# One 128-row tile for the last query rows of two heads, in an attention and mixer kernel

## The chip, the cores and the metric

The kernel runs on one core of one Trainium2 chip. The metric is the device time of one execution in microseconds (us); the median of the runs is what is compared.

## The reference

Causal attention with a forget-gate bias, then two mixers on its output. B = 4 batches, H = 8 heads, S = 576 positions, D = 64.

```python
cum  = np.cumsum(np.maximum(s, 0.0), axis=-1)
bias = -(cum[:, :, :, None] - cum[:, :, None, :])
scores = np.where(causal, -1e9, q @ k.T / np.sqrt(D) + np.minimum(bias, 0.0))
attn = np.exp(scores - scores.max(-1)); attn /= attn.sum(-1) + 1e-9
x = attn @ v                                  # [B, S, 512]
xk, xr = mu * x + (1 - mu) * x_prev           # one mu each
y = sigmoid(xr @ w_r) * (np.maximum(xk @ w_k, 0) ** 2 @ w_v)
u = y + (np.maximum(y.T @ w_tok1, 0) @ w_tok2).T
out = u + np.maximum(u @ w_ch1, 0) @ w_ch2
```

All data are float32.

## The kernel before

Products are made in the fp32r format of TensorE: a number is split into a high part (fp32r) and a low part, and two or three matmuls stand for one.

**Attention.** The 576 query rows of a head are five tiles: four of 128 rows (j = 0 to 3) and a last one of 64 (j = 4, `TAIL` = 64). Batch 0 goes through other functions (`early`, `late`) that the change leaves alone, but for one view. Batches 1 to 3 are 24 "visits" of one head each, and a pair (visit i, i + 1, i even) shares its loads. An "item" (i, j) is one query tile: `scores` (L286) makes two matmuls for each part of the row (L296 and L297; for j = 4 the 576 keys are two parts of 288), DVE masks them and takes the row maximum while it copies them to SBUF (L271), ACT makes the exponential (L281), POOL and DVE the reciprocal of the sum (L282, L283), and POOL scales the row (L284). `transposes` (L411) turns P in blocks of 128 keys (L421), ACT writes the high part of the result (L449 into `PT`), DVE the low part (L450). `values` (L452) multiplies with the split V in two passes: c = 0 for query rows 0 to 255 after j = 1, and c = 1 for rows 256 to 575 (`CM` = 320 columns) after j = 4; its matmuls are on L473. ACT and DVE then write the result into `xt` (L479, L480).

**Buffers.** Three PSUM tiles for scores (`ps_s`), two for transposes (`ps_t`), one for values (`ps_v`). `PT` has one buffer for the high and one for the low part, `X1`, `X2` (operands of the scores) one for even and one for odd visits. q and k of a pair come raw in four pieces (`load`, L228), are split into `HL` by ACT (L75) and POOL (L235) in `split`, and go from there by DMA to the operands of a visit in `place` (L261 to L264). `HL` has one buffer. V of a pair comes raw into `VS` in three DMAs (`load_v`, L240 and L242) after the tail of the even visit, and is split by DVE (L77) and POOL (L253) in `split_v` in the odd visit. These DMAs, and the stores of the mixer (L539), are all issued by SP, one after the other.

**Order.** Every piece of work has a place on a line of priorities, `at(N0 + n + ...)`, with n the number of the item; scores at n, transposes at n + 1.5, values at n + 2. The matmuls of the first mixer (`up`, `gate`, `down`; 40 units a batch, L107 through `products`) are dealt out over the items: batch 0's second half over the items of batch 1, batch 1's over those of batch 2, and so on, from the third item of a batch at the earliest. A scheduler takes the pieces by priority when its own timeline says they are ready, and so fixes the order on each engine before the run. After the last item come the mixer of batch 3 and the second mixer, which is TensorE work almost without a break.

Of the kernel before, what the change touches and what calls it, by code (L numbers as in the profile page):

```python
# [8 lines left out]
F32 = mybir.dt.float32  # L9
# [15 lines left out]
def attention_moe_mixer(  # L25
# [29 lines left out]
    QC = 256  # L55
# [71 lines left out]
    VS = v_p.tile([128, NS, 2 * D], F32, name="VS")  # L127
# [3 lines left out]
    FIRST = QC + 128  # L131
    BLK = [CM * k for k in range(NS - 1)] + [CM * (NS - 2) - (128 * (NS - 1) - QC)]
# [6 lines left out]
    def pt_tile(slot, dtype=F32):  # L139
        return pt_p.tile([128, (NS - 1) * CM], dtype, tag=f"PT{slot}", name=f"PT{slot}")  # L140
# [8 lines left out]
    def constants():  # L149
# [4 lines left out]
        make_identity(nc, ident)  # L154

# [47 lines left out]
    items = [(i, j) for i, (g, js, w) in enumerate(visits) for j in js]  # L203
# [33 lines left out]
    def load_v(i):  # L237
        b, h = divmod(visits[i][0], H)
        n = S // 128
        nc.sync.dma_start(out=VS[:, 0:n], in_=v[b, 0:128 * n, h * D:(h + 2) * D].rearrange("(t p) d -> p t d", p=128))  # L240
        for r in (0, TAIL):
            nc.sync.dma_start(out=VS[r:r + TAIL, n], in_=v[b, 128 * n:S, h * D:(h + 2) * D])  # L242

    def split_v(i):
        y = (i // 2) % 2
        if i < 4:
            VV[y] = v_tile(y, F32R)
        for t0, t1 in ((0, NS // 2), (NS // 2, NS)):
            hi = VV[y][:, t0:t1].rearrange("p t (x d) -> p t x d", d=D)[:, :, 0:4:3, :]
            lo = VV[y][:, t0:t1, D:3 * D].rearrange("p t (e d) -> p t e d", d=D)  # L250
            vs = VS[:, t0:t1].rearrange("p t (e d) -> p t e d", d=D)
            copy("D", hi, vs)
            nc.gpsimd.tensor_tensor(out=lo, in0=vs, in1=f32(hi), op=ALU.subtract)  # L253
# [14 lines left out]
    def softmax_max(j, ps, P, mx, x, c0, c1):  # L268
        m = min(128, S - 128 * j)
        q0 = 128 * j  # L270
        nc.vector.tensor_tensor_reduce(  # L271
            out=P[0:m, c0:c1], in0=ps[0:m, 0:c1 - c0], in1=maskc[0:m, 512 - q0 + c0:512 - q0 + c1],
# [4 lines left out]
    def softmax(j, P, mx, x):  # L277
        m = min(128, S - 128 * j)
        w = 128 * j + m
        sm = st_p.tile([128, 2], F32, tag="sum", name="sum")  # L280
# [5 lines left out]
    def scores(i, j):  # L286
        m = min(128, S - 128 * j)
        w = 128 * j + m
        x1, x2 = xs(i)
# [3 lines left out]
        parts = [(0, w)] if w <= 512 else [(0, w // 2), (w // 2, w)]  # L293
# [117 lines left out]
    def transposes(i, j):  # L411
# [23 lines left out]
        for r, k0, k1 in ((128, 0, nf), (TAIL, nf, nk)):  # L435
            if k0 == k1:
                continue
# [571 lines left out]
```

## Time and profile before

| What | us |
|---|---|
| Median of three runs (878.01 to 887.47) | 878.74 |
| The profiled execution | 877.69 |
| Its span, first to last instruction | 875.9 |
| PE busy, DVE, ACT, POOL | 846.1, 498.7, 460.7, 355.1 |
| First and last L296 matmul (scores of batches 1 to 3) | 121.1, 418.7 |

The span is cut by the profile into what each engine does. PE is TensorE's matmuls, PEld its weight loads, DVE the vector engine, ACT the scalar engine, POOL GpSimd, SP the engine that only issues DMAs; "SPq" and "PEq" are an engine's sequencer. A matmul's recorded duration runs from its start to the modelled end of its way through the array, so durations overlap: what a matmul costs in a stream is the step from its start to the next one's start.

### The profile page before, as it was taken

The numbers are of one execution on the slowest core, as the hardware profiler recorded it, in microseconds if no ns is written. First come the engines' busy times: TensorE is split into PE (matmuls) and PEld (weight loads), VectorE is DVE, ScalarE is ACT, GpSimd is POOL, SyncE is SP. The second block draws the span as 40 slices with busy tenths as digits, with TensorE's granted clock in tenths as the row PEclk, the third lists the DMA queues.
The fourth block names the chain that finished last, engine by engine and source line by source line (L and its number), as shares of the span: only waits on it lengthen the run. The fifth ranks groups of instructions, "written<-read, shape, count | busy, mean of one in ns | idle before, by whom it ended". The sixth has DMA issues, their size and how long they took to land.

```text
span 875.9 us, 17584 instructions
## 1 busy us (share of the span) xinstructions
PE 846.1 (97%) x6129; PEld 787.6 (90%) x6129; DVE 498.7 (57%) x1423; ACT 460.7 (53%) x1304; POOL 355.1 (41%) x622
## 2 busy tenths in 40 slices
PE   7999999998899999989999899999999999999998
PEld 5657779996799999989999899899999999999998
DVE  4878866667888657896469766961331222222221
ACT  3989757766877856769376774840310211211210
POOL 3765656755766745756256764730000000000000
PEclk7999999999989999999999999999999999999999
DMA  7953545556654536542234655562022112112100
GB/s 198 260 149 92 148 107 122 117 136 141 139 118 102 106 91 135 118 104 43 66 103 130 213 164 182 189 195 94 12 85 58 41 36 68 43 37 68 42 25 25
DMA packets 74888, 94.19 MB, mean 108 GB/s; under 512 B 10304, under 2 KB 58432, under 8 KB 74800
## 3 DMA queue, kind: packets, MB, share of 16 engines
q1 hardware_dynamic: 68352, 77.40, 34.1%
q0 software_dynamic: 4576, 15.08, 5.5%
q8 instruction: 49, 0.80, 0.4%
q10 hardware_dynamic: 1872, 0.59, 0.3%
q14 instruction: 39, 0.32, 0.1%
HBM read 56.50 MB, written 14.75 MB: 81 GB/s over the span
## 4 chain that ended last, share of the span: by engine, by line
PE 72%; DMA 8%; DVE 6%; issue 6%; ACT 4%; POOL 4%; SPq 1%; POOLq 0%; DVEq 0%; ACTq 0%
PE c L107 33%; PE h L107 8%; PE vd L107 6%; PE r L107 4%; PE t L421 3%; PE pv L473 3%; PE t L107 3%; PE pv L407 2%; PE s L378 2%; DMA X<-HL 2%; PE s L296 2%; PE s L297 2%; DMA raw<-in_moe_w_ch_dram 1%; DVE raw L596 1%; PE idle L162 1%
## 5 line engine op out<-in xcount | busy, mean ns | idle before, releaser
L848 ACT ACTIVATE HID<-c 128x256 fp32r<-128x256 f32 (+1 forms) x96 | 39.3, 410 | 220.6 <-PE c L107 220.5
L284 POOL TENSOR_SCALAR P<-P,sum 64x576 f32<-64x576 f32 (+4 forms) x160 | 102.9, 646 | 43.1 <-DVE sum L283 30.5
L107 PE MATMUL vd<-KK,WV 128*128 128x256 f32 (+1 forms) x768 | 120.1, 300 | 0.0
L107 PE MATMUL h<-XK,WK 128*128 128x320 f32 (+1 forms) x672 | 110.8, 307 | 2.8 <-ACT k L507 2.8
L281 ACT ACTIVATE P<-P,mx 64x576 f32<-64x576 f32 (+4 forms) x160 | 96.2, 603 | 27.8 <-DVE mx L271 24.9
L107 PEld LDWEIGHTS vd<-KK,WV 128*128 128x128 f32 x768 | 106.0, 188 | 3.4 <-issue 0.9
L107 PE MATMUL c<-HID,WV 128*128 128x256 f32 (+1 forms) x768 | 104.8, 291 | 0.0
L107 PE MATMUL c<-U,WK 128*128 128x256 f32 (+1 forms) x768 | 103.2, 292 | 0.6 <-DVE HID L849 0.6
L107 PEld LDWEIGHTS c<-HID,WV 128*128 128x128 f32 x768 | 100.6, 188 | 0.0
L107 PEld LDWEIGHTS h<-XK,WK 128*128 128x128 f32 x672 | 95.6, 192 | 5.5 <-ACT k L507 4.0
L107 PEld LDWEIGHTS c<-U,WK 128*128 128x128 f32 x768 | 98.6, 188 | 0.9 <-DVE HID L849 0.9
L849 DVE SCALAR_TENSOR_TENSOR HID<-c,HID 128x256 fp32r<-128x256 f32 (+1 forms) x96 | 43.8, 456 | 81.1 <-ACT HID L848 81.0
L913 DVE TENSOR_TENSOR ut<-c,ut 128x256 f32<-128x256 f32 (+1 forms) x32 | 14.7, 458 | 119.3 <-PE c L107 104.7
L271 DVE CUSTOM_DVE_ANT_0 P<-s,maskc 64x288 f32<-64x288 f32 (+4 forms) x160 | 74.3, 472 | 13.4 <-PE idle L162 4.4
L510 POOL TENSOR_TENSOR KK<-k,KK 128x256 fp32r<-128x256 f32 (+1 forms) x64 | 56.3, 882 | 12.3 <-ACT k L509 10.7
L107 PE MATMUL r<-XR,WR 128*128 128x320 f32 (+1 forms) x384 | 60.3, 299 | 0.0
L282 POOL TENSOR_SCALAR sum<-sum 128x1 f32<-128x1 f32 (+1 forms) x160 | 35.5, 222 | 60.2 <-ACT P L281 50.0
L421 PE MATMUL t<-ident,P 128*128 128x128 f32 (+1 forms) x360 | 53.4, 263 | 4.3 <-DVE PT L450 2.4
L107 PE MATMUL c<-HID,WR 128*128 128x256 f32 (+1 forms) x384 | 54.8, 291 | 0.0
L107 PEld LDWEIGHTS r<-XR,WR 128*128 128x128 f32 x384 | 52.7, 189 | 0.2
L107 PE MATMUL c<-U,C1A 128*128 128x256 f32 (+1 forms) x384 | 52.8, 296 | 0.0
L235 POOL TENSOR_TENSOR HL<-qkr,HL 128x288 f32<-128x288 f32 x48 | 40.2, 848 | 30.8 <-ACT HL L75 30.4
(122 smaller groups left out, 1685.4 us busy)
## 6 DMA issues: line engine op xcount, KB each, us to landing
X<-HL SPq DMA_DIRECT2D x72, 288.0 KB
raw<-in_moe_w_ch_dram POOLq DMA_DIRECT2D x48, 256.0 KB, 3.5
qkr<-in_qk_dram SPq DMA_DIRECT2D x48, 144.0 KB
yt<-y_d SPq DMA_DIRECT2D x16, 288.0 KB
u_d<-yt SPq DMA_DIRECT2D x16, 288.0 KB
raw<-in_moe_w_k_dram SPq DMA_DIRECT2D x8, 512.0 KB
raw<-in_moe_w_v_dram SPq DMA_DIRECT2D x16, 256.0 KB
ut<-u_d SPq DMA_DIRECT2D x32, 128.0 KB
```

What stands on the lines that cost most here:

```text
L107: nc.tensor.matmul(ps, a, b, start=first and i == 0, stop=last and i == n - 1)
L235: nc.gpsimd.tensor_tensor(out=lo, in0=t, in1=hi, op=ALU.subtract)
L271: nc.vector.tensor_tensor_reduce(out=P[0:m, c0:c1], in0=ps[0:m, 0:c1 - c0], in1=maskc[0:m, 512 - q0 + c0:512 - q0 + c1], scale=-scale, sca ...
L281: nc.scalar.activation(out=P[0:m, 0:w], in_=P[0:m, 0:w], func=AF.Exp, bias=mx[0:m, x:x + 1], scale=-1.0, accum_out=sm[0:m, 0:1])
L282: nc.gpsimd.tensor_scalar(out=sm[0:m, 0:1], in0=sm[0:m, 0:1], scalar1=1e-9, scalar2=1.0, op0=ALU.add, op1=ALU.mult)
L284: nc.gpsimd.tensor_scalar(out=P[0:m, 0:w], in0=P[0:m, 0:w], scalar1=sm[0:m, 1:2], scalar2=1.0, op0=ALU.mult, op1=ALU.mult)
L296: nc.tensor.matmul(ps[0:m, 0:c1 - c0], x1[:, 0, q0:q0 + m], x1[:, 1, c0:c1], start=True, stop=False)
L421: nc.tensor.transpose(ps[0:r, p0 + m * k:p0 + m * k + m], P[0:m, 128 * k:128 * k + r], ident[0:m, 0:m])
L473: nc.tensor.matmul(ps[:, o:n], vv[:, k, :], part, start=(k == 0 and t == 0), stop=(k == nk - 1 and t == len(parts) - 1),)
L510: nc.gpsimd.tensor_tensor(out=kk[:, 1, m, 0:n], in0=t[:, 0:n], in1=f32(kk[:, 0, m, 0:n]), op=ALU.subtract)
L848: nc.scalar.activation(out=hi, in_=ps, func=AF.Relu)
L849: nc.vector.scalar_tensor_tensor(out=lo, in0=ps, scalar=0.0, in1=f32(hi), op0=ALU.max, op1=ALU.subtract)
```

## The change

It touches batches 1 to 3 alone, apart from three small instructions at the start.

- The two 64-row tiles of a pair become one tile of 128 rows, worked at the even visit's j = 4: rows 0 to 63 are the even head's last queries, rows 64 to 127 the odd head's. The odd visit has four items. There are 108 items, and the mixer units are dealt out over them.
- Its scores come in parts of 512 and 64 keys instead of two of 288. For each part the odd head's two matmuls write 128 rows (its last 128 queries), then the even head's two overwrite rows 0 to 63.
- The 64 keys of the second part have a mask of their own, `maskp`, made at the start by a memset and a copy on POOL and a DMA on ACT's queue.
- One transpose of 128 x 128 for each of four key blocks, and one for the last 64 keys, into a PSUM tile of its own.
- A row of `PT` is 384 wide instead of 320 (`PW`): even tail, j = 2, j = 3, odd tail. Each head reads 320 of it. For the even head the block k = 3 comes in two pieces (64 and 128 columns) for each part, so its c = 1 pass has 11 matmuls instead of 9, and the result goes to `xt` in two DVE instructions.
- Raw V comes in two parts, key blocks 0 and 1, then 2 to 4, through a `VS` of three blocks instead of five. Part 0 is loaded at the even visit's j = 2 and split at its j = 4, behind that the load of part 1 is issued, and part 1 is split at the odd visit's j = 2.

```diff
-    VS = v_p.tile([128, NS, 2 * D], F32, name="VS")
+    VS = v_p.tile([128, (NS + 1) // 2, 2 * D], F32, name="VS")
+    maskp = v_p.tile([128, TAIL], BF16, name="maskp")
+    PW = CM + TAIL
-        return pt_p.tile([128, (NS - 1) * CM], dtype, tag=f"PT{slot}", name=f"PT{slot}")
+        return pt_p.tile([128, (NS - 1) * PW], dtype, tag=f"PT{slot}", name=f"PT{slot}")
+        nc.gpsimd.memset(maskp, 0.0)
+        nc.gpsimd.tensor_copy(maskp[0:TAIL], maskc[0:TAIL, 512:512 + TAIL])
+        nc.scalar.dma_start(out=maskp[TAIL:2 * TAIL], in_=maskc[0:TAIL, 512:512 + TAIL])
-    items = [(i, j) for i, (g, js, w) in enumerate(visits) for j in js]
+    items = [(i, j) for i in range(len(visits)) for j in range(NS - i % 2)]
+    PER = len(items) // (B - 1)
-    def load_v(i):
+    def load_v(i, c):
...
-    def split_v(i):
+    def split_v(i, c):
...
     def scores(i, j):
-        parts = [(0, w)] if w <= 512 else [(0, w // 2), (w // 2, w)]
+        parts = [(0, 128 * j), (128 * j, w)] if pair else [(0, w)]
         for x, (c0, c1) in enumerate(parts):
             ps = ps_s.tile([128, 512], F32, tag="s", name="s")
+            for e in (1, 0) if pair else (0,):
+                x1, x2 = xs(i + e)
+                n, a = (TAIL * (1 + e), S - TAIL * (1 + e)) if pair else (128, q0)
+                nc.tensor.matmul(ps[0:n, 0:c1 - c0], x1[:, 0, a:a + n], x1[:, 1, c0:c1], start=True, stop=False)
+                nc.tensor.matmul(ps[0:n, 0:c1 - c0], x2[:, 0, a:a + n], x2[:, 1, c0:c1], start=False, stop=True)
...
     def transposes(i, j):
+        if j == NS - 1:
+            tail = ps_t.tile([128, 512], F32, tag="t", name="t")
+            nc.tensor.transpose(tail[0:TAIL, 0:128], P[:, 128 * j:128 * j + TAIL], ident)
...
     def values(i, c):
+            todo = [(k, t[:, PW * k + f:PW * k + f + CM], 0) for k in range(NS - 2) for t in PT.values()]
+            for t in PT.values():
+                if e:
+                    todo.append((NS - 2, t[:, z + 3 * TAIL:z + PW], 2 * TAIL))
+                else:
+                    todo.append((NS - 2, t[:, z:z + TAIL], 0))
+                    todo.append((NS - 2, t[:, z + 3 * TAIL:z + CM], 3 * TAIL))
+            todo.append((NS - 1, PT[0][:, z + TAIL + f:z + 2 * TAIL + f], (CM - TAIL) * e))
...
+                    if j == 2:
+                        load_v(i + 2, 0)
                     if j == NS - 1:
-                        load_v(i + 2)
+                        split_v(i + 2, 0)
+                        load_v(i + 2, 1)
...
+            if j == 2:
                 with at(N0 + n + 0.3):
-                    split_v(i + 1)
+                    split_v(i + 1, 1)
...
-            if j == NS - 1:
+            if j == NS - 1 - i % 2:
                 values(i, 1)
```

## Rows read from the trace of the kernel before

**Rows 1.** Stretches of 25 us: busy time (count) by engine, clock, DMA share, GB/s.

```profile
200.00:225.00 25.00, 20.92 (x129) 17.60 (x129) 19.63 (x72) 18.03 (x53) 16.12 (x33) 0.93 0.55 128
225.00:250.00 25.00, 22.69 (x154) 20.81 (x154) 19.02 (x67) 20.78 (x64) 19.54 (x36) 0.86 0.68 153
...
350.00:375.00 25.00, 22.00 (x178) 20.68 (x177) 21.77 (x64) 18.67 (x59) 19.07 (x32) 1.00 0.51 117
```

**Rows 2.** A stretch counted for the mixers' matmuls (L107) alone: PE, PEld, clock, DMA.

```profile
210.00:227.00 17.00, 0.51 (x3) 0.36 (x3) 0.90 0.52 121
```

**Rows 3.** PE's waits, 175 to 430 us: total us, times, longest.

```profile
PE s L296 <- DVE mx L271: 3.1, 5, 1.6
PE pv L473 <- DVE xt L480: 2.8, 3, 1.6
PE t L421 <- DVE PT L450: 2.4, 2, 2.1
...
PE s L297 <- DMA X<-HL: 0.6, 1, 0.6
```

**Rows 4.** Timeline of PE, 290 to 300 us: start, duration, what, count.

```profile
289.76 0.60 PE L421 MATMUL t<-ident,P 128*128 128x128 f32 x4
290.12 0.98 PE L107 MATMUL h<-XK,WK 128*128 128x320 f32 x5
290.93 0.58 PE L473 MATMUL pv<-PF,VV 128*128 128x256 f32 x4
...
292.46 0.52 PE L421 MATMUL t<-ident,P 64*128 64x64 f32 x5
292.90 1.88 PE L107 MATMUL h<-XK,WK 128*128 128x320 f32 x11
294.62 0.34 PE L296 MATMUL s<-X 128*128 128x384 f32 x1
...
294.96 0.39 PE L296 MATMUL s<-X 128*128 128x512 f32 x1
295.20 0.39 PE L297 MATMUL s<-X 128*128 128x512 f32 x1
...
295.67 0.29 PE L297 MATMUL s<-X 128*64 128x288 f32 x1
295.80 0.89 PE L107 MATMUL h<-XK,WK 128*128 128x320 f32 x5
296.53 0.31 PE L473 MATMUL pv<-PT,VV 128*128 128x320 f32 x1
...
296.97 1.14 PE L473 MATMUL pv<-PT,VV 128*128 128x320 f32 x8
297.94 0.98 PE L107 MATMUL h<-XK,WK 128*128 128x320 f32 x5
298.76 0.38 PE L421 MATMUL t<-ident,P 128*128 128x128 f32 x2
```

**Rows 5.** Groups by form, 121 to 430 us: busy us, mean ns, idle before.

```profile
L271 DVE CUSTOM_DVE_ANT_0 P<-s,maskc,mx 64x288 f32<-64x288 f32 x24 | 12.0, 500 | 0.9 <-PE s L297 0.7
L271 DVE CUSTOM_DVE_ANT_0 P<-s,maskc 128x512 f32<-128x512 f32 x24 | 16.3, 679 | 0.1
L450 DVE TENSOR_TENSOR PT<-t,PT 128x256 fp32r<-128x256 f32 x24 | 9.9, 412 | 1.7 <-ACT PT L449 1.6
L450 DVE TENSOR_TENSOR PT<-t,PT 128x512 fp32r<-128x512 f32 x24 | 16.4, 682 | 4.3 <-ACT PT L449 4.2
L281 ACT ACTIVATE P<-P,mx 64x576 f32<-64x576 f32 x25 | 19.4, 774 | 10.3 <-DVE mx L271 10.2
L284 POOL TENSOR_SCALAR P<-P,sum 64x576 f32<-64x576 f32 x25 | 19.6, 785 | 5.5 <-DVE sum L283 3.9 <-PE s L296 0.6 <-PE pv L473 0.5
```

**Rows 6.** Timeline of SP's DMA issues, 210 to 228 us: start, duration, what, count.

```profile
212.34 1.07 SPq L264 DMA_DIRECT2D X<-HL  x1
213.46 2.93 SPq L242 DMA_DIRECT2D VS<-in_v_dram  x2
```

More of the change, by code (lines that the diff above doesn't have):

```diff
@@ L266, in attention_moe_mixer, with softmax_max @@
     pst = {}
-    def softmax_max(j, ps, P, mx, x, c0, c1):
-        m = min(128, S - 128 * j)
+    def softmax_max(j, ps, P, mx, x, c0, c1, mask=None):
         q0 = 128 * j
+        m = 128 if mask is not None else min(128, S - 128 * j)
+        if mask is None:
+            mask = maskc[:, 512 - q0 + c0:512 - q0 + c1]
         nc.vector.tensor_tensor_reduce(
-            out=P[0:m, c0:c1], in0=ps[0:m, 0:c1 - c0], in1=maskc[0:m, 512 - q0 + c0:512 - q0 + c1],
+            out=P[0:m, c0:c1], in0=ps[0:m, 0:c1 - c0], in1=mask[0:m],
             scale=-scale, scalar=3.0e38 if x == 0 else mx[0:m, x - 1:x],
@@ L275, in softmax_max, with softmax @@
         )
-    def softmax(j, P, mx, x):
+    def softmax(j, P, mx, x, pair=False):
         m = min(128, S - 128 * j)
         w = 128 * j + m
+        m = 128 if pair else m
         sm = st_p.tile([128, 2], F32, tag="sum", name="sum")
@@ L286, in scores @@
     def scores(i, j):
-        m = min(128, S - 128 * j)
-        w = 128 * j + m
-        x1, x2 = xs(i)
+        pair = j == NS - 1
+        w = 128 * j + (TAIL if pair else 128)
+        m = 128
         q0 = 128 * j
@@ L292, in scores @@
         mx = st_p.tile([128, 2], F32, tag="mx", name="mx")
-        parts = [(0, w)] if w <= 512 else [(0, w // 2), (w // 2, w)]
+        parts = [(0, 128 * j), (128 * j, w)] if pair else [(0, w)]
         for x, (c0, c1) in enumerate(parts):
             ps = ps_s.tile([128, 512], F32, tag="s", name="s")
-            nc.tensor.matmul(ps[0:m, 0:c1 - c0], x1[:, 0, q0:q0 + m], x1[:, 1, c0:c1], start=True, stop=False)
-            nc.tensor.matmul(ps[0:m, 0:c1 - c0], x2[:, 0, q0:q0 + m], x2[:, 1, c0:c1], start=False, stop=True)
-            softmax_max(j, ps, P, mx, x, c0, c1)
-        softmax(j, P, mx, x)
+            for e in (1, 0) if pair else (0,):
[3 more added lines that the diff above has]
+                nc.tensor.matmul(ps[0:n, 0:c1 - c0], x2[:, 0, a:a + n], x2[:, 1, c0:c1], start=False, stop=True)
+            softmax_max(j, ps, P, mx, x, c0, c1, None if not pair else maskp if x else maskc[:, 0:c1])
+        softmax(j, P, mx, x, pair)
         pst[i, j] = P
@@ L411, in transposes @@
     def transposes(i, j):
-        m = min(128, S - 128 * j)
+        m = 128
         P = pst.pop((i, j))
-        nk = j + 1
+        nk = min(j + 1, NS - 1)
         if not 0 < j < QC // 128:
@@ L645, in attention_item @@
                     if x == 3:
-                        load_v(0)
+                        load_v(0, 0)
             if h == H - 1 and j == 3:
                 with at(N0 + n + 0.2):
-                    split_v(0)
+                    split_v(0, 0)
+                    load_v(0, 1)
+            if h == H - 1 and j == 4:
+                with at(N0 + n + 0.2):
+                    split_v(0, 1)
             if h == H - 2 and j == 2:
```

93 lines of the change are left out of this document (46 added, 47 removed).

## The prediction

> **What bounds the kernel now.** I read the busy times first. PE is busy for 846.1 of 875.9 us (the table), so work taken from DVE, ACT or POOL buys nothing unless it shortens one of PE's few stalls, and PE's own work counts in full. Then I looked for those stalls with the busy time in stretches of 25 us. Batches 1 to 3 run from about 121 to 430 us, and three stretches there stand out: PE lacks 4.1, 2.3 and 3.0 us of 25, 9.4 together [rows 1]. In the first two the mean granted clock is 0.93 and 0.86: at the lower level, 1.2 GHz, for 0.07 x 25 / 0.5 = 3.5 us and 7.0 us, which costs half of that, 5.2 us. The prize of an attention stage without these stalls is 9.4 + 5.2 = 14.6 us, 1.7%.
>
> What the stalls are: between 210 and 227 us only three mixer matmuls ran, 0.51 us of PE's time [rows 2]. One batch's mixer units were used up and the next batch's were not ready, so PE lived on attention alone and saw the full latency of the softmax chain. The table of PE's waits names who ended most of the idle time: DVE, freeing a PSUM tile after the row maximum (3.1 us), after the write to `xt` (2.8), after the low part of `PT` (2.4), 8.3 us together; one wait of 0.6 us was for a DMA from `HL` [rows 3]. In the three stretches DVE is busy for 19.6, 19.0 and 21.8 us of 25, 81% [rows 1]: loaded enough that a queue forms.
>
> **The change on PE.** The price of a matmul is the step from its start to the next start, as the timeline shows it, and what the run behind it is late. A mixer matmul of 320 columns steps by (296.53 - 295.80) / 5 = 0.146 us [rows 4].
>
> Scores. Before, a pair makes 8 matmuls of 64 rows by 288 keys, at 295.80 - 295.67 = 0.13 each: 1.04 us. After, it makes 4 of 512 keys, at 295.20 - 294.96 = 0.24, which is 0.96, and 4 of 64 keys. The trace has no score matmul of 64 columns. The nearest rows are the end of a c = 1 pass: five of 320 columns, two of 192 and one of 64 take 297.94 - 296.97 = 0.97, and the five behind them 0.82 instead of 0.73; so the three short ones cost 0.24 + 0.09 = 0.33, 0.11 each, though their 448 columns would take 0.20 at the mixer's rate [rows 4]. A matmul of 64 columns then costs between its columns, 0.03, and 0.11. As half of these have weights of half the width, I take 0.08: 0.32 a pair. Scores: +0.24 a pair (+0.04 to +0.36), +2.9 us over 12 pairs (+0.5 to +4.3).
>
> Transposes. Five of 64 rows take 292.90 - 292.46 = 0.44 and make the eleven behind them 1.72 instead of 1.61: 0.55, a pair 1.10. Four of 128 rows take 290.12 - 289.76 = 0.36 and the five behind them 0.81 instead of 0.73: 0.44 [rows 4]. The fifth, of the last 64 keys, has half the weights: 0.03 to 0.11, and I take 0.11, the step of its neighbours: 0.55. Saved 0.55 a pair, 6.6 us (to 7.6).
>
> Values. The even head ends on five short matmuls instead of three with the same 448 columns: at 0.11 each +0.22 a pair, at columns alone nothing. I take the dear end, since three of the five are as narrow as the dearest one in the rows: +2.6 us (0 to 2.6). PE in all: 2.9 - 6.6 + 2.6 = -1.1 us, from -7.1 to +0.3. What halving the transposes gives, the narrow pieces nearly take back.
>
> Here the Trainium skill would count otherwise. Its page "TensorE: Matmul & The Clock Gate", Part 2, "Back-to-back issue gap", gives an isolated matmul of up to 64 columns a floor of 25 ns, by which the narrow pieces would be almost free and PE would come out at its low end; it adds that a stream with a weight load for each matmul is dearer, and the 0.33 us for three here speaks for the stream.
>
> **The change beside PE.** DVE: four mask passes of 0.50 us and two low parts of 0.41 a pair become one pass of 0.68 for 512 keys, one of 64 keys (between nothing and 0.50, I take 0.25) and one low part of 0.68: 2.82 - 1.61 = 1.2 us less a pair, 14 us; the 64 x 64 low parts and the second write to `xt` about cancel. ACT loses one exponential of 0.77 us a pair, POOL one scaling of 0.79, 9 us each [rows 5]. A pair takes (418.7 - 121.1) / 12 = 25 us (the table), so DVE falls by 5% of the time. None of it is on PE's path outside the stalls. Inside them a queue at 81% that loses 5% of the time and a tenth of its items may lose a third of its waits: -3.1 us of the 9.4. The lower clock came with these same stalls; if half of it is avoided, -2.6. I see no reason for more: in the attention-only stretch the next operands must come through `HL`, which this change doesn't touch, and SP, which sends them, had just issued X's last piece at 212.34 and then V for 2.93 us [rows 6].
>
> Moved and added. The V load is four DMAs a pair instead of three, and its second part now waits, in SP's own queue, for the DVE and POOL passes over the first; behind it stand the `place` DMAs of the next even head and the mixer's stores. An issue costs 1.1 to 1.5 us of SP here [rows 6]. That is hidden while the operands land before PE has gone through the odd head; I take nothing, and the price without that cover is the last rival. The splits of V no longer come in one lump, which is no loss. The pair tile takes both `ps_t` tiles, so the last transpose waits until DVE is done with j = 3's, one item earlier than today; this adds to the kind of the 2.4 us row, and is why I take no more than a third off [rows 3]. At the start come two small POOL instructions and a DMA on ACT's queue, each on 64 rows by 64 columns; PE waits there for the first scores' chain, so I take nothing; a DMA issue at most, 1 us, if it stands in that chain.
>
> Sum: -1.1 - 3.1 - 2.6 = -6.8 on the profiled 877.69, which is 1 us under the median: 870.9, and I say 871.
>
> **Rivals.**
> *The stalls stay*, as they are set by mixer units that aren't ready and by `HL`: 877.7 - 1.1 = 877. For it: three mixer matmuls in 17 us [rows 2], which a shorter tail doesn't mend.
> *The stalls mostly go*: four fifths of 14.6, so 877.7 - 1.1 - 11.7 = 865. For it: DVE ended 8.3 us of them. Against it: DVE itself stands in a chain with ACT and POOL.
> *A transpose holds PE for its whole recorded time*: two are recorded as 0.38 us, of which one step is about 0.11, so one lasts 0.27. Ten a pair would be 2.7 us and five 1.35: -16.2 instead of -6.6, and 871 becomes 861. The timeline is against it: five start within 0.44 us [rows 4]. The Trainium skill's page "TensorE: Matmul & The Clock Gate", Part 4, "PE-mode transpose", gives about 275 ns for one within a kernel, which would stand behind this reading; by the starts here that is a latency.
> *Slower: the wait in SP's queue.* With four items in the odd visit the next even head's operands must land an item sooner, and they queue behind a load that waits for POOL. It decides if SP has no slack, as just after 212 us, where PE waited 0.6 us for X [rows 3, 6]. The price is then the added issue and the wait for the split, 1.0 to 1.5 us in each of 11 pairs: 877.7 - 1.1 + 11 to 16.5, 888 to 893; I take 890.
>
> **How the numbers follow.** The forecast, 871 (866 to 876): 0.42. Stalls stay, 877: 0.22. Stalls mostly go, 865: 0.16. Long transposes, 861: 0.02. SP's queue, 890: 0.18. One per cent, 8.8 us, is about what a measurement of this kernel can tell from no change. Faster by more (under 870): 0.16 + 0.02 and somewhat less than half of the forecast's 0.42, 0.37. Slower by more (over 887.5): the SP case, 0.17. Within: 0.46. The range goes from 861, the stalls mostly gone with PE's terms near their low ends, to 886, which leaves out the SP case.
>
> **What would show it.** Right: 60 transposes fewer on L421, DVE's busy time down by about 14 us, ACT's and POOL's by 9 or more; narrow pieces that step by about 0.1 us; the stretch without mixer matmuls still there, with shorter waits for DVE. Wrong on the slow side: PE waiting for DMA X<-HL in many pairs, and SP at the second V load. Wrong on the fast side: the clock at 1.00 through the whole stage and DVE's waits gone. An order of instructions that the scheduler lays quite differently, with new gaps in the weight conversion after 430 us, would put both sums beside the point.

## The result, and the profile after

The changed kernel takes 891.08 us (median of 6 runs, 889.55 to 892.23), the kernel before 878.54 in the same comparison: ratio 1.0139, 95% interval 1.0099 to 1.0179. It is slower by 12.5 us. I had said 871, with 861 to 886 as the range and 0.17 for slower. The profiled run of after took 892.23 us, the longest of its six, and spans 890.5. Executions that ran far longer than the rest of their kernel, or over 1.5% longer at a lower granted clock, are left out of all medians and ratios (two of e4, one each of e13 and e18), and since the profiles of e13 and e18 are of such a one, only waits are read from them.

The page of after, first its engines (busy us, share, instructions), then the three stretches of [rows 1]:

```profile
PE 851.3 (96%) x6093; PEld 794.4 (89%) x6093; DVE 488.5 (55%) x1351; ACT 451.8 (51%) x1256; POOL 340.1 (38%) x600
```

```profile
200.00:225.00 25.00, 20.71 (x125) 18.04 (x124) 17.71 (x58) 14.49 (x40) 14.43 (x28) 0.92 0.63 145
225.00:250.00 25.00, 21.19 (x138) 19.40 (x137) 18.19 (x63) 18.56 (x56) 16.53 (x33) 0.87 0.55 130
350.00:375.00 25.00, 24.00 (x189) 22.56 (x188) 19.89 (x61) 22.55 (x67) 18.34 (x34) 1.00 0.61 131
```

The lighter engines came nearly as forecast: DVE -10.2 us (14 were forecast), ACT -8.9, POOL -15.0. Yet in the first two stretches PE lacks 8.1 us of 50 where before it lacked 6.4 [rows 1], though DVE is now busy for less of the time. (After is some 8 us behind by then, so the stretches don't hold quite the same work.) Where the time is by place: the last score of batch 0 (the `late` tiles) starts at 126.2 us instead of 118.3, the first `c` matmul of the second mixer at 553.0 instead of 539.0, and from there to the end both take the same 337 us. So some 8 us are lost in batch 0, which the change touches only by its mask and, at its end, by the first loads of V, and 6 between there and the second mixer.

**Batch 0.** The clearest view is SP's waits from 17 to 34 us (total us, times, longest). Before:

```profile
SPq L363 <- DMA ext_d<-e: 2.1, 1, 2.1
```

After:

```profile
SPq L373 <- DMA ext_d<-e: 6.7, 1, 6.7
```

And SP's issues of after (start, duration, what, count):

```profile
22.15 0.37 SPq L598 DMA_DIRECT2D raw<-in_moe_w_k_dram  x1
29.29 0.28 SPq L373 DMA_DIRECT2D X<-ext_d  x1
...
31.81 0.39 SPq L378 DMA_DIRECT2D VV<-in_v_dram  x1
...
33.99 1.10 SPq L598 DMA_DIRECT2D raw<-in_moe_w_v_dram  x2
```

SP stands for 6.7 us in front of the load of X from `ext_d`, and the loads of VV and of `w_v` come behind it. In the kernel before they stood ahead of it:

```profile
23.80 0.51 SPq L363 DMA_DIRECT2D VV<-in_v_dram  x1
...
28.71 1.07 SPq L358 DMA_DIRECT2D X<-ext_d  x3
...
31.49 1.18 SPq L578 DMA_DIRECT2D raw<-in_moe_w_v_dram  x2
```

ACT, which converts the weights, then waits for them: 4.1 us in all from 36 to 60 us, 0.7 before. What follows is seen at 50 to 80 us (stretches of 10 us of after, columns as in [rows 1]; the clock is the number behind the five engines):

```profile
50.00:60.00 10.00, 7.54 (x25) 3.58 (x24) 8.34 (x21) 8.89 (x22) 5.45 (x6) 0.69 0.64 194
60.00:70.00 10.00, 8.82 (x32) 4.84 (x31) 6.33 (x16) 7.64 (x19) 4.69 (x8) 0.67 0.19 59
70.00:80.00 10.00, 10.00 (x48) 7.30 (x48) 6.13 (x17) 5.12 (x15) 4.43 (x6) 0.79 0.09 27
```

The same of the kernel before:

```profile
50.00:60.00 10.00, 8.33 (x31) 4.03 (x31) 9.27 (x24) 9.74 (x24) 5.19 (x7) 0.85 0.34 101
60.00:70.00 10.00, 10.00 (x73) 8.31 (x72) 7.39 (x22) 7.16 (x23) 6.54 (x10) 0.98 0.38 110
70.00:80.00 10.00, 10.00 (x57) 6.42 (x56) 8.03 (x24) 8.73 (x27) 5.11 (x10) 1.00 0.33 96
```

In after PE idled 1.75 us up to 47.9 and 2.04 us up to 54.9, waiting for ACT and for DVE's row maximum, and at 53.8 the granted clock went to its lower level, 1.2 GHz. It is 0.31, 0.33 and 0.21 below one in the three stretches, so 17 us of these 30 were at half speed, against 3.4 before.

**Batches 1 to 3.** DVE's copy of V into VV (L77, 384 columns: V's second part) is the group that changed most (busy, mean ns, idle just before it, and what ended that). The kernel before, and after:

```profile
L77 DVE CAST VV<-VS 128x384 fp32r<-128x384 f32 x11 | 6.0, 546 | 0.4 <-PE pv L473 0.4
```

```profile
L77 DVE CAST VV<-VS 128x384 fp32r<-128x384 f32 x12 | 6.6, 550 | 10.0 <-DMA VS<-in_v_dram 9.9
```

One of these waits in after's timeline (POOL, SP, DVE; the bracket is the idle time before):

```profile
195.15 0.74 POOL L262 TENSOR_TENSOR VV<-VS,VV 128x256 fp32r<-128x256 f32 x1
195.92 0.39 SPq L248 DMA_DIRECT2D VS<-in_v_dram  x1
...
200.30 0.55 DVE L77 CAST VV<-VS 128x384 fp32r<-128x384 f32 x1 [2.60 <-DMA VS<-in_v_dram]
```

POOL's pass over the first part ends at 195.89, SP issues the second load into the same blocks at 195.92, DVE's copy of the data starts 4.3 us later, and DVE, whose order is fixed before the run, has stood 2.60 us in front of it; the next row maximum is behind it. In the chain of waits from 192 to 262 us the transfers of V have the largest share, 15.7%.

### The profile page after: what moved, and what is told of

Its sections match the earlier page's. It is cut to its first block, busy times and chain, and to the rows that moved or that the text cites. A ratio compares the mean times of both kernels' runs of the same rounds, so it can differ in the third digit from the quotient of the medians.

```text
span 890.5 us, 17382 instructions
## 1 busy us (share of the span) xinstructions
PE 851.3 (96%) x6093; PEld 794.4 (89%) x6093; DVE 488.5 (55%) x1351; ACT 451.8 (51%) x1256; POOL 340.1 (38%) x600
## 4 chain that ended last, share of the span: by engine, by line
PE 66%; DMA 10%; DVE 9%; issue 6%; ACT 5%; POOL 4%; SPq 0%; POOLq 0%; DVEq 0%; ACTq 0%
PE c L107 32%; PE h L107 8%; PE vd L107 5%; PE t L107 3%; PE r L107 3%; PE pv L494 3%; PE s L393 2%; DMA raw<-in_moe_w_ch_dram 2%; PE pv L422 2%; DMA raw<-in_moe_w_tok_dram 2%; DMA VS<-in_v_dram 2%; PE t L436 2%; DVE P L282 2%; PE s L312 1%; PE s L311 1%
## 5 line engine op out<-in xcount | busy, mean ns | idle before, releaser
L107 PE MATMUL vd<-KK,WV 128*128 128x256 f32 (+1 forms) x768 | 124.0, 304 | 1.0 <-ACT e L542 0.6
L296 POOL TENSOR_SCALAR P<-P,sum 128x128 f32<-128x128 f32 (+4 forms) x148 | 94.9, 644 | 49.9 <-DVE sum L295 38.8
L107 PEld LDWEIGHTS vd<-KK,WV 128*128 128x128 f32 x768 | 108.3, 191 | 5.5 <-issue 2.2
L107 PE MATMUL h<-XK,WK 128*128 128x320 f32 (+1 forms) x672 | 104.7, 302 | 1.2 <-ACT k L527 1.2
L293 ACT ACTIVATE P<-P,mx 128x128 f32<-128x128 f32 (+4 forms) x148 | 86.7, 587 | 36.7 <-DVE mx L282 30.0
L107 PE MATMUL c<-HID,WV 128*128 128x256 f32 (+1 forms) x768 | 104.8, 291 | 0.0
L107 PE MATMUL c<-U,WK 128*128 128x256 f32 (+1 forms) x768 | 103.2, 292 | 1.3 <-DVE HID L877 1.3
L107 PEld LDWEIGHTS c<-HID,WV 128*128 128x128 f32 x768 | 100.6, 188 | 0.0
L107 PEld LDWEIGHTS c<-U,WK 128*128 128x128 f32 x768 | 98.6, 188 | 1.8 <-DVE HID L877 1.6
L107 PEld LDWEIGHTS h<-XK,WK 128*128 128x128 f32 x672 | 93.3, 189 | 2.6 <-ACT k L527 1.9
L282 DVE CUSTOM_DVE_ANT_0 P<-s,maskc 128x128 f32<-128x128 f32 (+4 forms) x148 | 72.1, 496 | 29.1 <-PE t L436 8.0
L107 PE MATMUL r<-XR,WR 128*128 128x320 f32 (+1 forms) x384 | 60.1, 299 | 0.0
L294 POOL TENSOR_SCALAR sum<-sum 128x1 f32<-128x1 f32 (+1 forms) x148 | 30.7, 207 | 63.9 <-ACT P L293 56.5
L436 PE MATMUL t<-ident,P 128*128 128x128 f32 x288 | 49.0, 285 | 6.3 <-POOL P L296 4.0
L107 PE MATMUL c<-HID,WR 128*128 128x256 f32 (+1 forms) x384 | 54.8, 291 | 0.0
L107 PEld LDWEIGHTS r<-XR,WR 128*128 128x128 f32 x384 | 52.9, 188 | 0.4
L107 PE MATMUL c<-U,C1A 128*128 128x256 f32 (+1 forms) x384 | 52.8, 296 | 0.3 <-ACT U L926 0.3
L107 PEld LDWEIGHTS c<-U,C1A 128*128 128x128 f32 x384 | 51.5, 190 | 0.5 <-ACT U L926 0.5
```

What stands on the lines that cost most here:

```text
L107: nc.tensor.matmul(ps, a, b, start=first and i == 0, stop=last and i == n - 1)
L282: nc.vector.tensor_tensor_reduce(out=P[0:m, c0:c1], in0=ps[0:m, 0:c1 - c0], in1=mask[0:m], scale=-scale, scalar=3.0e38 if x == 0 else mx[0 ...
L293: nc.scalar.activation(out=P[0:m, 0:w], in_=P[0:m, 0:w], func=AF.Exp, bias=mx[0:m, x:x + 1], scale=-1.0, accum_out=sm[0:m, 0:1])
L294: nc.gpsimd.tensor_scalar(out=sm[0:m, 0:1], in0=sm[0:m, 0:1], scalar1=1e-9, scalar2=1.0, op0=ALU.add, op1=ALU.mult)
L296: nc.gpsimd.tensor_scalar(out=P[0:m, 0:w], in0=P[0:m, 0:w], scalar1=sm[0:m, 1:2], scalar2=1.0, op0=ALU.mult, op1=ALU.mult)
L436: nc.tensor.transpose(ps[0:r, p0 + m * k:p0 + m * k + m], P[0:m, 128 * k:128 * k + r], ident[0:m, 0:m])
```

## The experiments

All are timed against the kernel before, which was measured beside them each time. Theory A: the DMA of the mask turns over SP's early loads. Theory C: V in two parts costs a wait, in SP's queue. Theory E: the pair tile gains on PE, but PE then waits for the next operands (X, by way of `HL`). Another letter in an expectation is the rival that is described beside it there.

| kernel | median us | ratio to before | 95% interval |
|---|---|---|---|
| after | 891.1 | 1.0139 | 1.0099 to 1.0179 |
| e1: before + mask, unused | 882.5 | 1.0041 | 1.0013 to 1.0069 |
| e2: after, mask without a DMA | 884.5 | 1.0058 | 1.0028 to 1.0088 |
| e3: after, mask's DMA on POOL's queue | 882.4 | 1.0041 | 1.0017 to 1.0065 |
| e5: after, mask in eight DMAs | 892.9 | 1.0126 | 1.0082 to 1.0171 |
| e9: after, order pinned | 884.9 | 1.0094 | 1.0057 to 1.0131 |
| e10: before, order turned | 881.7 | 1.0029 | 1.0002 to 1.0057 |
| e4: before, V in two parts | 882.9 | 1.0038 | 1.0010 to 1.0066 |
| e17: the same with room for V | 879.0 | 0.9995 | 0.9962 to 1.0027 |
| e13: e3 with two buffers of `e` | 882.3 | 1.0058 | 1.0027 to 1.0089 |
| e18: e3, second V load on POOL's queue | 883.9 | 1.0041 | 1.0009 to 1.0072 |
| e12: e13 with room for V | 878.3 | 0.9999 | 0.9968 to 1.0031 |
| e8: e13 with V whole | 877.6 | 0.9959 | 0.9929 to 0.9990 |
| e16: after with room for V | 888.8 | 1.0095 | 1.0066 to 1.0125 |
| e11: e8, pair from even operands | 876.3 | 0.9981 | 0.9952 to 1.0010 |
| e14: e8, HL chain meant sooner | 876.7 | 0.9991 | 0.9965 to 1.0018 |
| e15: before, HL chain meant sooner | 881.5 | 1.0045 | 1.0001 to 1.0088 |

e14 and e15 left every engine's instructions in the order that they had, so they are second measurements of e8 and of the kernel before. They lie 0.0032 and 0.0045 from the first: a ratio that stands alone carries little under half a per cent here, whatever its interval, and below I lean on groups of kernels that agree.

### The mask's DMA and SP's early loads

**e1**, the kernel before with the three instructions of the mask added and nothing that uses it.

```diff
+    maskp = v_p.tile([128, TAIL], BF16, name="maskp")
...
+        nc.gpsimd.memset(maskp, 0.0)
+        nc.gpsimd.tensor_copy(maskp[0:TAIL], maskc[0:TAIL, 512:512 + TAIL])
+        nc.scalar.dma_start(out=maskp[TAIL:2 * TAIL], in_=maskc[0:TAIL, 512:512 + TAIL])
```

> The kernel before with nothing added but the set-up of the pair mask at the start (memset and copy on POOL, one DMA on ACT's queue; the mask is not used). Theory A (the early loss of some 8 us in the changed kernel comes from the order of SP's DMAs, which one more DMA on a hardware queue at the start turns over): SP sits idle from about 22.5 to 29 us in front of the X load from ext_d, the weight loads come 3 to 8 us later, scores of batches 1 to 3 start at about 129 instead of 121 us, and the time is 885 to 888 against about 878.5. Theory B (the early loss comes from the wider PT rows, the smaller VS or the V loads): no change, 877 to 880.

Measured 1.0041, 882.5 us, less than the 885 to 888 that I expected, though SP stands for 6.7 us in front of `ext_d` as in after. **e2** and **e3** take the DMA off ACT's queue: e2 makes the mask on POOL with a memset and a select for each half, without a DMA, and e3 issues the DMA from POOL's queue.

```diff
-        nc.scalar.dma_start(out=maskp[TAIL:2 * TAIL], in_=maskc[0:TAIL, 512:512 + TAIL])
+        nc.gpsimd.dma_start(out=maskp[TAIL:2 * TAIL], in_=maskc[0:TAIL, 512:512 + TAIL])
```

> The changed kernel with the pair mask made by POOL alone, without a DMA; all else as changed. Theory A: SP's early order is that of the kernel before again, scores of batches 1 to 3 start at about 121 us, and 8 of the 12.5 us come back: about 883. Theory B: nothing comes back, 890 to 892. Theory C (the SP queue's wait for the split of V is what costs, in the attention stage): 890 or so in any case, with PE's waits for X from HL as in the changed kernel.

> The changed kernel with the mask's DMA issued by POOL instead of ACT; the DMA and its data are the same. Theory A: a DMA on POOL's queue does not shift the hardware queues' turn, SP's early order is that of the kernel before, about 883 as with the mask made without a DMA. If the DMA itself or what it moves cost the time: 890 to 892.

Measured 1.0058 and 1.0041: 6.6 and 8.7 us of the 12.5 are back. In e3 the mask's DMA is still there, so it is neither its bytes nor the mask, but the queue that it is issued on. SP's early waits of e3:

```profile
SPq L378 <- DMA ext_d<-e: 0.5, 1, 0.5
```

**e5** cuts the DMA in eight, so that later DMAs get the same turns as before among the eight semaphores that SP's and ACT's early DMAs signal one after the other (the "lanes"; more on them at e9).

```diff
-        nc.scalar.dma_start(out=maskp[TAIL:2 * TAIL], in_=...)
+        for r in range(TAIL, 2 * TAIL, TAIL // 8):
+            nc.scalar.dma_start(out=maskp[r:r + TAIL // 8], in_=...)
```

> The changed kernel with the mask's rows brought by eight DMAs of eight rows on ACT's queue in place of one of 64, so that the DMAs issued behind it are dealt to the same hardware lanes as in the kernel before. Theory A (one DMA more turns over the order in which SP issues the first loads; not the DMA's own work): the order is nearly that of the kernel before again, and although seven DMAs are added the time falls by 6 to 9 us against the changed kernel, to 882 to 885. Rival (the DMA's own time on ACT's queue, or its traffic, delays the start): eight are worse than one, 891 or more.

A miss: 892.9. The wait for `ext_d` is down to 0.8 us, but the first four loads of X now go out over 6.73 us instead of 2.66 (the fourth, at 14.52, waits for semaphore 109, which a piece of the mask issued at 8.47 signals), and all that follows is late. The edit removes one delay and makes another, so it speaks for neither side.

**e9** holds three loads of X behind VV's in the changed kernel; **e10** turns the order over in the kernel before, by `turned` around the later loads of X, q and k, VV, V, `w_v` and the last pieces of `w_k`.

```diff
+        with tc.issue_after(v_dma[1].ins):
+            for h in range(3):
+                ext_load(h)
...
+    def turned(h, do, *a):
+        with tc.issue_after(ext_dma[h].ins):
+            do(*a)
```

> The changed kernel as it is, with the mask's DMA on ACT's queue, but with SP's early order put back by hand: the three loads of X from ext_d are held behind the loads of VV in SP's queue (order of issue only, no wait is added). Theory A (the loss at the start is the order alone): the last late score comes by 120 to 123 us instead of 126, and the time is 882 to 885. Rival (the mask's DMA on ACT's queue, or the other hardware lanes that it deals, cost the time by themselves): 889 to 892, as the changed kernel.

> The kernel before, with no mask and no added DMA, but with SP's early order turned to that of the changed kernel: the first load of X from ext_d stands ahead of the loads of VV, w_v and the later pieces of w_k. Theory A: SP stands still in front of that load until about 29 us, the last late score comes 3 to 8 us later than 118.3 us, and the time is 882 to 886. Rival (the order is harmless without the mask's DMA): 878 to 880.

e9 takes 884.9, as Theory A had it, and its last late score starts at 120.5 us. Its six runs lie far apart, though, from 881.3 to 890.6, and by the ratio only 0.45 of after's 1.39 per cent are back. And its SP row says that the order wasn't the whole of it:

```profile
SPq L383 <- DMA ext_d<-e: 6.0, 1, 6.0
```

Now the load of VV stands for the write of `ext_d`, with which it shares no data. What they share is a semaphore. In the traces the early DMAs of SP and ACT signal eight semaphores in turn (100, 102, 103 and 105 to 109), and a DMA first waits for the last use of its own; such a turn is what I call a lane. In e9 the write of `ext_d` that ACT issues at 19.40 us signals 108, and the load of VV at 29.11 waits for 108. The mask's DMA on ACT's queue takes one of the turns (107, which in the kernel before is that of a load of `HE`); in e3, on POOL's queue, it has a semaphore outside them. So there are two ways to the same stand: through the data (after, e1, e10) and through the lane (e9). The short waits shown above, 2.1 us before and 0.5 in e3, are of the second kind as well, since L363 and L378 are loads of VV.

e10, with a stand of 5.7 us and no mask, came to 1.0029, under what I expected and no more than a repeat's spread; its last late score starts at 119.4. The wait alone is cheap in the kernel before; with the pair tile the DMA on ACT's queue costs 7 to 10 us (after against e2 and e3, e16 against e12). Why it costs more there isn't settled, as the scheduler lays the whole of batch 0 otherwise. Part of it is the lower clock behind the stand. The profile of e16, which has the same DMA on ACT's queue and is described below, is of its fastest run (883.2, its median is 888.8). SP's load of X from `ext_d` goes out at 27.70 us there, yet the clock is back from 60 us on:

```profile
50.00:60.00 10.00, 9.02 (x25) 4.09 (x26) 8.46 (x24) 9.25 (x22) 5.47 (x7) 0.66 0.50 152
60.00:70.00 10.00, 9.60 (x72) 7.80 (x71) 6.62 (x22) 7.23 (x22) 5.54 (x9) 1.00 0.29 85
```

That is 6.8 us at the lower level from 50 to 80 us, against 17 in after and none in e3, and the last late score starts at 120.1 instead of after's 126.2. The 10 us less at half speed are worth 5 us. (PE's order is the same in both up to the 262nd matmul, at 62.9 us in e16 and 66.8 in after.)

### V in two parts

**e4** is the kernel before with the loads and splits of V as in the change.

```diff
-    VS = v_p.tile([128, NS, 2 * D], F32, name="VS")
+    VS = v_p.tile([128, (NS + 1) // 2, 2 * D], F32, name="VS")
...
+                    if j == 2:
+                        load_v(i + 2, 0)
                     if j == NS - 1:
-                        load_v(i + 2)
+                        split_v(i + 2, 0)
+                        load_v(i + 2, 1)
...
```

> The kernel before with V in two parts through the smaller VS (same places of load and split as in the changed kernel), the last tiles of 64 rows and the mask left as they were. Theory C (SP's queue waits for the split of V's first part): slower by 1.0 to 1.5 us a pair, 890 to 893, with PE waiting for X from HL in several pairs. Theory D (the V load is off the path, and what the attention stage lost comes from the pair tile or from a new order): 877 to 880.

Measured 1.0038, between what Theory C (890 to 893) and its rival (877 to 880) had. **e17** keeps the two loads and the places of the splits, but gives the second part blocks of its own; **e12** and **e13** do this with the pair tile, **e13** being the control that makes the last edit, the buffer of `e` that pays for the room, alone (e17 leaves it out).

```diff
-    VS = v_p.tile([128, (NS + 1) // 2, 2 * D], F32, name="VS")
+    VS = v_p.tile([128, NS, 2 * D], F32, name="VS")
-        nc.sync.dma_start(out=VS[:, 0:n], in_=...)
+        nc.sync.dma_start(out=VS[:, t0:t0 + n], in_=...)
...
-        e = act["sm"].tile([128, CM], F32, tag="e", name="e", bufs=3)
+        e = act["sm"].tile([128, CM], F32, tag="e", name="e", bufs=2)
```

> The kernel before with V loaded by four DMAs and split at two places as in the changed kernel, in its own tile of five blocks, so that no load waits for a pass. Theory C (the small tile's wait is the cost, the added DMA and the moved passes are not): 878 to 880, as before. Rival (the parts themselves cost): 882 to 885, as with the small tile.

> As the kernel with V whole (three DMAs, 877.6): VS of five blocks, two buffers of e, the mask's DMA on POOL's queue; but V is loaded by four DMAs and split in two parts at the changed kernel's places. The second part has blocks of its own, so its load waits for no pass over the first. Theory C (what V in two parts costs is the wait in SP's queue): 877 to 879, as with V whole. Rival (it is the added DMA and the other places of loads and passes): 881 to 884, as the pair tile with V in two parts through the small tile, 882.4.

> The pair tile with V in two parts through the small tile and the mask's DMA on POOL's queue (882.4), with the gate tile e cut from three buffers to two and nothing else. If the room for V is what gave the 3.7 us: 881 to 885, no change. Rival (two buffers of e are the better number by themselves): 877 to 879.

Room gives 3.9 us to the kernel before (882.9 to 879.0) and 4.0 to the pair tile (882.3 to 878.3); the buffer alone gives nothing (882.4 to 882.3). **e18** tries the mechanism that I had named, SP's queue.

```diff
+        q = nc.gpsimd if c else nc.sync
-        nc.sync.dma_start(out=VS[:, 0:n], in_=...)
+        q.dma_start(out=VS[:, 0:n], in_=...)
```

> The pair tile with V in two parts through the small tile and the mask's DMA on POOL's queue (882.4 and, with two buffers of e, 882.3), with V's second load issued from POOL's queue, where the pass that it waits for is the instruction before it, so that nothing in SP's queue stands behind it. Theory C (what is queued behind the load on SP pays): 877 to 880. Rival (the second part itself comes too late, or POOL pays for issuing its three DMAs): 882 or more.

883.9, nothing back. That alone doesn't clear SP's queue, since POOL now has to issue three DMAs a pair. But for X, which stands behind that load on SP, PE waits no longer with the small tile (4.0 us in after, 3.4 in e3) than with room (5.0 in e8, 5.4 in e12). After's rows, SP's wait at V's load from 125 to 430 us and PE's for X from 128 to 444:

```profile
SPq L248 <- POOL VV L262: 20.5, 10, 2.9
```

```profile
PE s L312 <- DMA X<-HL: 4.0, 2, 2.3
```

What differs is DVE. The row of V's second copy in e18, then in e12:

```profile
L77 DVE CAST VV<-VS 128x384 fp32r<-128x384 f32 x12 | 6.6, 551 | 13.2 <-DMA VS<-in_v_dram 11.5 <-issue 1.5
```

```profile
L77 DVE CAST VV<-VS 128x384 fp32r<-128x384 f32 x11 | 6.0, 545 | 0.3 <-DMA y_d<-e 0.3
```

This wait sorts the kernels: 6.8 to 11.7 us for the DMA in all of after, e2, e3, e4, e5, e9, e13 and e18, which have the small tile, none in those that have room (e8, e12, e16, e17). The first kind are the slower ones, by 4 to 6 us in the comparisons above: without the mask's DMA on ACT's queue, five with the small tile lie at 1.0038 to 1.0058 (e2, e3, e4, e13, e18) and five with room at 0.9959 to 0.9999 (e8, e11, e12, e14, e17). (e15, which has the whole tile, lies at 1.0045, which shows how far a single one can be off.) PE feels it. From the first value matmul of batches 1 to 3 (the first with `PF`) to the second mixer's first `c` matmul, DVE ended 12.1 and 10.8 us of PE's waits in e3 and e2, against 3.9 and 4.5 in e8 and e12 (12.6 in e4, 9.3 in e17), and with the pair tile this stretch takes 402.5 and 402.3 us against 399.7 and 399.3.

So it is shown that the small tile costs these 4 to 6 us, and that PE then waits for DVE. It isn't shown that all of it is DVE's stand at the copy: the small tile also changes the scheduler's order. e12 has e8's order on PE and e17 that of the kernel before, while e4 and e13 have orders of their own.

**e16** gives room to the changed kernel itself.

> The changed kernel with its mask's DMA on ACT's queue (so with its early order of SP), and room for V alone: VS of five blocks, its second part in blocks of its own, two buffers of e. If the two costs add up: 5 to 7 us under the changed kernel, 884 to 886. Rival (the early order hides or takes over what V's wait costs): 889 to 892.

888.8: by the medians 2.3 us back, by the ratios 0.44%, 3.9 us; less than I expected, with the wait on DVE gone. From after, either order of repair ends at the same place (891.1, 882.4, 878.3 or 891.1, 888.8, 878.3); whether what one costs depends on the other can't be told from the spread of repeats.

### The pair tile itself

**e8** is the pair tile with neither fault: V whole in its tile of before, the mask's DMA on POOL's queue, two buffers of `e`.

> The pair tile without V in two parts: V is loaded by three DMAs into a tile of five blocks as before, the mask's DMA stands on POOL's queue, and the room is taken from the gate tile e of the softmax-mixer glue, two buffers instead of three. If V in two parts costs what it cost alone (3.4 us) and the pair tile is neutral: 878 to 881, the same as before. If the pair tile itself is worth what I forecast for PE and the stalls (4 to 7 us): 872 to 876, faster than both. Rival (V's parts cost nothing beside the pair tile, or the third buffer of e was needed): 882 or more.

877.6 and, as e14 measured it again, 876.7: ratios 0.9959 and 0.9991, with e12 and e11 0.9999 and 0.9981. Together about 0.2% faster than before, 1 to 3 us, and not told from no change by any one of them but e8. PE's groups from 137 to 430 us (busy us, mean ns, idle before) show that the tile does its work. Before:

```profile
L421 PE MATMUL t<-ident,P 128*128 128x128 f32 (+1 forms) x354 | 52.2, 263 | 4.3 <-DVE PT L450 2.4 <-POOL P L284 1.3
L296 PE MATMUL s<-X 128*128 128x512 f32 (+1 forms) x135 | 45.1, 338 | 3.4 <-DVE mx L271 3.1
L297 PE MATMUL s<-X 128*128 128x512 f32 (+1 forms) x135 | 42.9, 323 | 0.6 <-DMA X<-HL 0.6
...
L473 PE MATMUL pv<-PT,VV 128*128 128x320 f32 (+2 forms) x207 | 36.6, 294 | 0.9 <-DVE xt L480 0.7 <-DVE PT L450 0.2
L473 PE MATMUL pv<-PF,VV 128*128 128x256 f32 (+1 forms) x96 | 15.3, 281 | 2.7 <-DVE xt L480 2.6
```

e8:

```profile
L433 PE MATMUL t<-ident,P 128*128 128x128 f32 x285 | 46.6, 278 | 2.0 <-POOL P L293 1.8
L308 PE MATMUL s<-X 128*128 128x256 f32 (+3 forms) x135 | 43.4, 329 | 0.4 <-DVE mx L279 0.4
L309 PE MATMUL s<-X 128*128 128x128 f32 (+3 forms) x136 | 42.3, 317 | 5.0 <-DMA X<-HL 5.0
...
L491 PE MATMUL pv<-PT,VV 128*128 128x320 f32 (+1 forms) x231 | 36.4, 292 | 1.0 <-ACT PT L451 0.4 <-DVE PT L452 0.3
L491 PE MATMUL pv<-PF,VV 128*128 128x256 f32 (+1 forms) x96 | 15.8, 272 | 3.0 <-DVE xt L497 2.4 <-ACT PT L461 0.6
L448 PE MATMUL t<-ident,P 128*64 128x128 f32 x12 | 3.4, 283 | 0.0
```

The wait for DVE's row maximum fell from 3.1 us to 0.4, and X rose from 0.6 to 5.0. These X waits end at 142.5, 208.2 and 226.1 us, each at the first tile of an even head, which comes one tile sooner now that the odd visit has four.

**e11** makes the odd head's half of the pair from the even head's operands (first edit), **e14** and **e15** were to bring X one tile sooner (second edit).

```diff
-                x1, x2 = xs(i + e)
+                x1, x2 = xs(i)
...
-                    if j >= NS - 2:
-                        split(j - NS + 2)
+                    if j >= NS - 3:
+                        split(j - NS + 3)
...
```

> The kernel with V whole and the mask's DMA on POOL's queue (877.6), with one word changed: the odd head's half of a pair's tile is made from the even head's operands, so that this tile doesn't need the odd head's X (the last 64 queries of odd heads in batches 1 to 3 are then wrong). Theory E (the pair tile asks for the odd head's X one tile too soon, and the HL chain ends where DVE's queue ended before): the three X waits of 1.4 to 2.2 us go and the time falls by 2 to 5 us, to 873 to 876. Rival (they only stand in for other waits, since X comes when it comes and the odd head's own tiles wait next): 877 to 879.

> The pair tile with V whole (877.6), and the HL chain moved one tile ahead: the four splits of the next pair stand at tiles 2, 3 and 4 of the even head and tile 0 of the odd one (instead of 3, 4, 0 and 1), and the place DMAs of the next even head at tile 0 of the odd one (instead of 1). Theory E, corrected (the odd visit has four tiles now, so the next even head's first score comes a tile sooner than its X): the X waits of 5.0 us mostly go, and the time falls by 2 to 5 us, to 873 to 876. Rival (the chain's length holds, not its place in the order; or ACT's and POOL's splits then stand ahead of the softmax passes that PE waits for): 877 to 880.

> The same move of the HL chain in the kernel before, where PE waits 0.6 us for X. Theory E: nothing to be had, 878 to 880, so that what the move gives the pair tile is owed to the pair tile. Rival (an earlier X helps any kernel by as much): 874 to 876.

e11 changes no order and hardly the time, and its three X waits are where they were: I had looked at the wrong tile, as it is the next even head that waits and not the pair. In e14 and e15 the new places changed no order either; I take it that the scheduler had already put each split and load as early as it could. So the place in the list isn't what holds X. e8's trace says what does at the first of the three waits (SP and PE):

```profile
135.83 0.27 SPq L267 DMA_DIRECT2D X<-ext_d  x1
...
137.48 0.82 SPq L270 DMA_DIRECT2D X<-HL  x1
```

```profile
135.86 0.19 PE L309 MATMUL s<-X 128*64 128x64 f32 x1
...
142.49 0.33 PE L309 MATMUL s<-X 128*128 128x128 f32 x1 [1.42 <-DMA X<-HL]
```

The pair tile is the last reader of the even head's X, which has one buffer. PE ends it at 135.9, SP issues the next even head's X into that buffer from 135.83 to 138.30, as PE lets go of its parts, and PE can use it 4.2 us later. The second wait is of the same kind: PE ends the pair tile at 200.9, SP issues from 201.39 to 203.93, and PE goes on at 208.2. At the third the pieces from `HL` are issued only from 219.63 on, though PE has let go of X at 216.6. So much is read from the trace; no run gave X a second buffer.

**e6** and **e7** were to take the X waits away altogether, in the kernel before and in e3, by sending the place DMAs to a scratch tensor; all later heads then use the first two heads' operands.

> The kernel before, with the scores of batches 1 to 3 always made from the operands of the first two heads: the place DMAs are still issued and still read HL, but write to a scratch tensor, so that PE never waits for X (the attention output of the later heads is then another). It gives what the kernel before pays for X. Theory E (the pair tile needs the odd head's X sooner, and PE now waits for the HL chain instead of for DVE): little is gained here, the time lies 0 to 4 us under the kernel before, 875 to 879. Rival (X costs both kernels alike): as much is gained here as in the twin of the changed kernel.

> The same on the changed kernel with the mask's DMA on POOL's queue (882.4 as measured), so that neither the early order nor X holds PE. Theory E: 4 to 8 us under the 882.4, 874 to 878, and at or under the twin made from the kernel before. Rival (the X waits only stand in for other waits, or what is lost lies in V's two parts on DVE, POOL and SP): 881 or more, and 3 us or more above the twin, as without this edit.

Both failed as experiments: 899.2 and 908.2 us. The DMAs now wait for one another, as they share the scratch (SP's waits of e6, 121 to 450 us):

```profile
SPq L267 <- DMA aside<-HL: 9.2, 12, 1.1
```

But about half of e6's loss comes before that, as its last late score already starts at 128.8 us instead of 118.3. What causes it stays open, and the two say nothing on X.

## Why the prediction was wrong

The step that failed is the paragraph "Moved and added", at both of its ends.

- *"At the start come two small POOL instructions and a DMA on ACT's queue ... I take nothing."* It cost 7 to 10 us. I priced the DMA's own time and looked for who waits for the mask. Nobody does; the loads that follow on SP wait instead, for the write of `ext_d`, and the clock falls behind that.
- *"That is hidden while the operands land before PE has gone through the odd head; I take nothing."* V's small tile cost 4 to 6 us, 2 to 4 in after. I had followed the load to SP's queue and asked what stands behind it there. The consumer is DVE's copy, which waits for the late data in DVE's queue, with the row maxima behind it (9.9 us in after); that added wait I didn't name at all.
- The rival "the wait in SP's queue" gave 890, near the time by luck, for its mechanism is not the one. SP did stand at V's load (20.5 us in after, above), but PE waited for X only twice, 4.0 us, not in many pairs. Its condition, operands needed an item sooner, did come true (X waits of 5.0 us in e8 against 0.6 [rows 3]), but as the price of the pair tile and not of V, and far under its 11 to 16.5 us.
- PE's own work: -1.1 us forecast. By the busy times of e8's groups above, transposes go from 52.2 to 50.0 us and scores from 88.0 to 85.7, with the values at 51.9 and 52.2: -4.2. By the steps from start to start, summed over the scores, transposes and values from the first PF value to the second mixer with idle time left out, it is -2.3 for scores, -4.2 for transposes and +1.5 for values, -5.0. So transposes gave less than the 6.6 (and the rival of long transposes, with 16.2, is out), values cost 1.5 instead of 2.6, and scores were wrong in sign. The narrow score pieces themselves were about right, 0.34 us in the pair shown against 0.32 (after's timeline, start and duration), 0.31 and 0.24 on average in after and e8:

```profile
308.54 0.28 PE L311 MATMUL s<-X 128*128 128x64 f32 x1
308.65 0.28 PE L312 MATMUL s<-X 128*128 128x64 f32 x1
308.76 0.22 PE L311 MATMUL s<-X 128*64 128x64 f32 x1
308.82 0.22 PE L312 MATMUL s<-X 128*64 128x64 f32 x1
308.88 1.12 PE L107 MATMUL h<-XK,WK 128*128 128x320 f32 x6
```

  The 0.13 us that I took for a 64-row score of the kernel before was read off one matmul and too cheap: over the 92 of them in the trace of this stretch the step is 0.155, 2.4 us more in 12 pairs. The narrow pieces cost 1.0 us less in e8 than forecast, and the scores of the other tiles 1.3 us less than before; why stays open.
- The stalls: -3.1 forecast. In e8's stretches PE lacks 5.8, 3.8 and 2.0 us, in place of 4.1, 2.3 and 3.0:

```profile
200.00:225.00 25.00, 19.24 (x129) 15.99 (x127) 20.52 (x74) 18.35 (x53) 16.05 (x36) 1.00 0.68 148
225.00:250.00 25.00, 21.25 (x158) 20.49 (x158) 17.46 (x58) 19.17 (x61) 17.31 (x32) 0.93 0.53 118
350.00:375.00 25.00, 23.03 (x187) 21.97 (x186) 23.97 (x64) 19.13 (x57) 19.39 (x32) 1.00 0.53 117
```

  By starts, PE's idle time from the first PF value to the second mixer is 20.2 us in e8 (19.2 in e14) against 16.6 (15.6 in e15): +3.6. The waits for DVE did shorten, and by more than the third that I took: DVE ended 10.8 us of them before and 3.9 in e8 (9.9 in e15, 4.2 in e14). But others came in their place: X from 0.6 to 5.0, a reload of `y_d` from nothing to 2.5, ACT's `e` from nothing to 2.0. That is where PE's gain went.
- The clock: -2.6 forecast. 1.00 and 0.93 in these stretches, so 3.5 us at the lower level instead of 10.5: -3.5. The second pair of profiles says about the same: 1.00 and 0.86 in e14, 7.0 us, against 0.87 and 0.86 in e15, 13.5 us: -3.2. So this term was nearly right.

These can't be added up as the forecast's terms were, for the steps from start to start already hold what the clock gives. The stretch from the first `PF` value to the second mixer as a whole takes 399.7 us in e8 against 402.3 before, and 400.6 in e14 against 403.2 in e15: -2.6 both times, of which -5.0 is PE's attention work and +3.6 its idle time in the first pair. That agrees with the -1 to -3 of the medians; the forecast was -6.8. So without the two faults the pair tile's gain has the direction of the forecast and less than half its size, since other waits took the place of DVE's; the 12.5 us lay in what came along to make room for it and to mask it.

## What to carry to other kernels

A transfer that is added to a scheduled kernel is priced by what it does to the queues and lanes of the others, not only by its own length: look at the order of the loads behind it, and try it on another queue before anything else. When a buffer is cut so that its second half must wait for the first half's last reader, ask which engine will stand in front of the late half, and what is queued there. And measure a program twice: here two such repeats lay 0.3 and 0.45% from the first, as much as this tile could give.

## What the runs showed of the hardware that I had not expected

A load of VV waited 6.0 us for a write of `ext_d` that it has no data in common with, as both have the same one of eight semaphores (e9); that is how the program is built, and not a matter of the data. Eight DMAs of 8 rows in place of one of 64 drew out four loads of SP behind them from 2.66 to 6.73 us (e5). The transfer of V's second part took 4.3 us from issue to use (after), and X's last piece 4.2 us from the end of its issue to its use (e8). And in batch 0 much the same early stand of SP came with 17 us at the lower clock in after's profile and 6.8 in e16's.
